# Stage 1 in row halves for two quarters, the last quarter's second stage in two halves, and a new order of issue

## The chip, the cores and the metric

The kernel runs on one core of a Trainium2 chip. A core has five engines with an instruction stream each: TensorE (PE in the profile, with its weight loads listed apart as PEld), VectorE (DVE), ScalarE (ACT), GpSimd (POOL) and SyncE (SP), which issues DMA transfers here. An engine works through its stream in order; between engines, semaphores say when a result is there or a buffer is free. The metric is the time of one execution on the device in microseconds, the median of several runs.

## The reference

Two layers in sequence, on 2048 positions of 512 channels, everything in float32:

```python
def _A_ref(u, ...):                       # S4D: a long convolution per channel
    P = exp((A * dt[:, None])[:, :, None] * pos)          # 512 x 128 x 2048, complex
    K = 2.0 * einsum("dn,dnl->dl", C, P).real             # the kernel of 2048 taps
    y = irfft(rfft(u_t, 2 * L) * rfft(K, 2 * L), 2 * L)[:, :, :L]
    return y + u * D_skip
def _B_ref(x, w_q, k1, k2, u, v):         # PEER: one expert of 256 for each of 32 heads
    q = einsum("nd,dhc->nhc", x, w_q)                     # 2048 x 32 x 256
    s1, s2 = q[..., :128] @ k1.T, q[..., 128:] @ k2.T     # 16 scores each
    e = argmax(s1) * 16 + argmax(s2)
    act = gelu(einsum("nd,nhd->nh", x, u[e]))
    return einsum("nh,nhd->nd", act, v[e])
h  = x + _A_ref(layernorm(x), ...)
h2 = h + _B_ref(layernorm(h), ...)
```

With one candidate per head the softmax is 1. The convolution of both layers' input needs all positions, so the second layer starts when the convolution is through.

## The kernel before, in words

**The first layer** runs over four quarters c of 128 channels, and within them over 32 chunks i of 16 channels (eight to a quarter, two to a piece kt of 32 channels).

For each chunk the taps are made from tables: P at position 64a + b is a product of a coarse power and a fine one. POOL adds the phases as integers (`pg`, in `phases`), and multiplies out the magnitudes (`mg` and `gf`, in `mags` and `tails`); for every fourth chunk it also makes the powers that the next four chunks need (`steps`, `bases`). ACT takes the sines and cosines of the phases into PSUM tiles `t`, named by k (0 coarse, 1 fine) and cosine or sine, DVE multiplies them onto the magnitudes, and PE sums over the 128 states (`kgen`, the tile `kps`: called the product of a chunk below). The tables `pg`, `mg` and `gf` have two buffers each: POOL may write the magnitudes of chunk i when the product of chunk i − 2 has been read.

The Fourier transforms are factored into two stages of matrix products, made for the taps (k) and for the input (u). Stage 1 (`stage1`, tiles s1u and s1k) takes a piece of 32 channels: eight groups g of four channels, 32 rows each, lie on the 128 partitions, and each group is multiplied with two constant matrices `c1_s[:, k]` (real and imaginary part) of 128 by 128, block-diagonal in the four channels. Two plan entries per piece make four groups each, and ACT copies each result (a PSUM bank) into the spectrum `yu` or `yk`:

```python
for k in range(2):
    T.matmul(ps[64 * k:64 * k + 64, g, :], lhs8(4 * n + g), c1_s[:, k], start=True, stop=True)
```

Each of these matmuls of float32 leaves two records in the trace: eight matmuls per entry, 16 records. Stage 2 (`stage2`, tiles s2u and s2yk) has eight operations k4 per quarter, each four matmuls of 128 by 128 (8 records) over the whole spectrum of the quarter, so it needs all four pieces of stage 1. The result for u is copied by ACT into `U`; the result for k is multiplied with `U` by DVE (`prod`). In the last quarter (c = 3) the last of three partial products is left to POOL (`rest`), which reads a copy that ACT makes (`part`). The inverse transform starts with `ia` (`k_ia`): eight operations n of 16 records, each over four groups of channels and the products of all k4. ACT (in the last quarter DVE too) turns the results into the tile `T`, and for the first three quarters SP stores it to DRAM (`t_d`).

In between, PE also projects the second layer's weights onto its keys: 32 pieces n (`w_piece`: the load of `wq` by SP, the product `wps`, a copy `wt`, a transposition `wpt`, a copy into `wh`, and a store per four pieces). The seven PSUM banks of the pool `psA` are shared by stage 1, stage 2, `ia`, the trigonometry and the projections.

**The second layer** runs over the positions: the inverse transform's second part (`ib`), the layer norm with a square on ACT, a product on PE and a sum `vs` on POOL, then for each half the scores (`sc`), the largest of 16 on DVE, the experts' activations, the counts and the output.

**The order.** Nothing is scheduled while the kernel is built: every step is an entry of a plan, with its engine, its dependencies and its buffers, and the table `ORDER` lists the 1728 entries by number. `Plan.run` issues them in that order, so each engine's stream is the table filtered by engine:

```python
for n in order:
    assert n not in done and done.issuperset(self.ops[n][4])
    done.add(n)
    self.ops[n][3]()
```

## Time and profile before

| | us |
|---|---|
| median of three runs (504.18 to 505.11) | 504.2 |
| the profiled execution | 504.94 |
| its span, first to last instruction | 503.2 |
| PE busy | 449.0 (89%) |
| weight loads busy (beside PE) | 390.3 (78%) |
| DVE busy | 407.8 (81%) |
| POOL busy | 325.5 (65%) |
| ACT busy | 298.3 (59%) |

Durations are worked out within the one profiled execution. In the rows of the profile, a time at the row's start is the start in microseconds from the beginning of the span, followed by the duration; then come the engine, the line of the kernel, the operation, and the output tile with `<-` its inputs. A bracket at the end says how long the engine had been idle just before and whose work ended that. In rows that group instructions, busy time and mean duration stand behind the bar, and idle time and its releaser behind the next. An instruction of PE overlaps the next one, so an operation's cost is read from the time between the first and last of its records, not from one record's duration.

Three places of the span matter here: the tables and products up to 263 us, the tail of the last quarter up to 298 us, and the second layer behind it.

### The profile page before, as it was taken

Reading aid. Unit: us, or ns where it says so; the run is one execution under the profiler, and the core shown is the slowest. Engines: PE = TensorE matmul, PEld = TensorE weight load, DVE = VectorE, ACT = ScalarE, POOL = GpSimd, SP = SyncE. Lnnn points to the kernel's source line nnn. Section 1 sums busy time; section 2 is a strip of 40 time slices with the busy share of each in tenths; the row PEclk is TensorE's granted clock in tenths of the full one; section 3 lists DMA queues with packets and bytes.
Section 4 is the critical chain, followed back from the end, with each engine's and each line's share of the span. In section 5 each row is a group of like instructions: output and inputs, shape, how many; then the busy total and the mean of one; then the engine's idle time right before and its main releaser. Section 6 shows DMA issues by size and latency. Waiting matters only on the chain.

```text
span 503.2 us, 16702 instructions
## 1 busy us (share of the span) xinstructions
PE 449.0 (89%) x7206; PEld 390.3 (78%) x7206; DVE 407.8 (81%) x708; ACT 298.3 (59%) x594; POOL 325.5 (65%) x344
## 2 busy tenths in 40 slices
PE   0266879999998999999998889999999999999985
PEld 0144568888997999889997787877878888787874
DVE  5998998899968998899745574888979686978984
ACT  4867799967987588967965362644043430416230
POOL 4989989999999999997824303572163516536130
PEclk9998799999999999999999899999999999999999
DMA  8959474234033300631017689310171311010012
GB/s 253 403 198 381 143 288 148 66 86 179 2 111 124 85 3 1 212 126 45 1 61 259 200 275 283 127 61 1 57 227 55 109 63 43 1 44 0 1 68 62
DMA packets 27362, 61.05 MB, mean 121 GB/s; under 512 B 7028, under 2 KB 14456, under 8 KB 26136
## 3 DMA queue, kind: packets, MB, share of 16 engines
q1 hardware_dynamic: 27136, 59.85, 34.9%
q8 instruction: 57, 0.93, 0.7%
q10 hardware_dynamic: 152, 0.13, 0.1%
q14 instruction: 17, 0.14, 0.1%
HBM read 46.08 MB, written 13.89 MB: 119 GB/s over the span
## 4 chain that ended last, share of the span: by engine, by line
PE 50%; DVE 22%; ACT 10%; POOL 10%; issue 4%; DMA 3%; SPq 1%; ACTq 0%; DVEq 0%; POOLq 0%
PE sc L1150 12%; PE ia L764 9%; DVE oh L1280 5%; PE s2yk L488 3%; PE xu L1157 3%; PE kps L690 3%; PE s2yu L488 3%; POOL pg L557 3%; PE s1u L471 3%; DVE st L232 2%; PE o L1327 2%; PE ib L1036 2%; PE cnt L1290 2%; ACT t L645 2%; POOL mg L594 2%
## 5 line engine op out<-in xcount | busy, mean ns | idle before, releaser
L557 POOL TENSOR_TENSOR pg<-PS 128x1024 int32<-128x1024 int32 x32 | 68.8, 2150 | 0.5
L588 POOL TENSOR_TENSOR mg<-TS 128x1024 f32<-128x1024 f32 x32 | 62.6, 1958 | 7.2 <-PE kps L690 4.5
L1280 DVE TENSOR_SCALAR oh<-idxb,ec_s 128x2048 bf16<-128x2048 bf16 (+1 forms) x72 | 50.3, 757 | 6.8 <-ACT idxb L1262 6.8
L764 PE MATMUL ia<-ca_s,U 128*128 128x128 f32 x256 | 50.6, 280 | 0.4 <-POOL U L743 0.4
L1060 POOL TENSOR_TENSOR vs<-hc 128x256 f32<-128x256 f32 x8 | 7.0, 872 | 62.6 <-ACT hc L1083 62.6
L1192 POOL TENSOR_TENSOR ks<-kq 128x512 f32<-128x512 bf16 x16 | 17.2, 1078 | 45.9 <-DVE kq L1186 44.8
L645 ACT ACTIVATE t<-t,halfpi 128x512 f32<-128x512 f32 x64 | 42.4, 662 | 2.1
L1150 PE MATMUL sc<-w_hi,hhi 128*128 128x480 f32 x128 | 42.4, 412 | 0.0
L644 ACT ACTIVATE t<-pg 128x512 f32<-128x512 int32 x64 | 38.9, 609 | 3.2 <-DVE gf L652 2.2
L764 PEld LDWEIGHTS ia<-ca_s,U 128*128 128x128 f32 x256 | 39.8, 196 | 0.6 <-POOL U L743 0.6
L647 ACT ACTIVATE t<-pg 128x512 f32<-128x512 int32 x64 | 38.2, 608 | 2.8 <-POOL pg L557 1.5
L764 PE MATMUL ia<-ca_s,yk 128*128 128x128 f32 x192 | 38.1, 280 | 0.4 <-DVE mg L664 0.4
L1150 PE MATMUL sc<-w_lo,hhi 128*128 128x480 f32 x128 | 38.4, 380 | 0.0
L1150 PE MATMUL sc<-w_hi,hlo 128*128 128x480 f32 x128 | 38.3, 380 | 0.0
L594 POOL TENSOR_TENSOR mg<-TS 128x512 f32<-128x512 f32 x32 | 37.4, 1170 | 0.4
L690 PE MATMUL kps<-mg 128*32 128x64 f32 x1024 | 34.0, 230 | 3.8 <-DVE mg L664 2.2
L488 PE MATMUL s2yk<-yk,c_s 128*128 128x128 f32 x256 | 34.7, 282 | 1.1 <-ACT yk L474 0.7
L471 PE MATMUL s1u<-c_s,xs 128*64 128x128 f32 x512 | 33.3, 277 | 2.5 <-DVE xs L508 1.6
L690 PE MATMUL kps<-gf 128*32 128x64 f32 x1024 | 33.7, 229 | 1.8 <-issue 1.8
L488 PEld LDWEIGHTS s2yk<-yk,c_s 128*128 128x128 f32 x256 | 30.6, 191 | 4.2 <-issue 1.4
L488 PE MATMUL s2yu<-yu,c_s 128*128 128x128 f32 x256 | 32.6, 279 | 0.3
L471 PEld LDWEIGHTS s1u<-c_s,xs 128*64 128x64 f32 x512 | 27.6, 137 | 5.4 <-DVE xs L508 1.7
(198 smaller groups left out, 1377.5 us busy)
## 6 DMA issues: line engine op xcount, KB each, us to landing
wq<-wq SPq DMA_DIRECT2D x25, 512.0 KB, 4.5
t_d<-T SPq DMA_DIRECT2D x24, 256.0 KB, 3.4
Tb<-t_d SPq DMA_DIRECT2D x8, 768.0 KB, 6.0
x<-xa SPq DMA_DIRECT2D x8, 512.0 KB, 5.6
xs<-xb SPq DMA_DIRECT2D x16, 256.0 KB, 5.3
xt<-xt SPq DMA_DIRECT2D x8, 512.0 KB, 4.8
out<-ob SPq DMA_DIRECT2D x7, 512.0 KB, 3.0
c_s<-wq SPq DMA_DIRECT2D x4, 512.0 KB, 8.3
```

Source lines behind the costliest of these rows:

```text
L471: T.matmul(ps[64 * k:64 * k + 64, g, :], lhs8(4 * n + g), c1_s[:, k], start=True, stop=True)
L488: T.matmul(ps[:, k, :], c2_s[:, kk, :], y[:, :, kk, :], start=True, stop=True)
L557: G.tensor_tensor(view(pg, 0, [[32, 2 * NC], [8, 4], [1, 8]]), view(t["PS"], 1024 + off, [[1, 2 * NC], [128, 4], [0, 8]]), view(t["PS"], 8 ...
L588: G.tensor_tensor(view(mg, 0, [[96, NC], [8, 8], [1, 8]]), view(ts, 512 + 8 * o, [[8, NC], [1, 8], [0, 8]]), view(ts, 8 * o, [[8, NC], [0, ...
L594: G.tensor_tensor(view(mg, 64, [[96, NC], [8, 4], [1, 8]]), view(ts, 1536 + o, [[1, NC], [64, 4], [0, 8]]), view(ts, 1024 + 8 * o, [[8, NC ...
L644: A.activation(p, pg[:, :, k], AF.Abs)
L645: A.activation(p, p, AF.Sin, scale=-SINSCALE, bias=halfpi)
L647: A.activation(p, pg[:, :, k], AF.Sin, scale=SINSCALE)
L690: T.matmul(kps[32 * q:32 * q + 32, 2 * g + h, :], m[:, d, 64:96], m[:, d, 0:64], start=(e == 0), stop=(e == 1))
L764: T.matmul(ps[:, g, :], t[:, 4 * n + g].rearrange("p a b -> p (a b)"), ca_s[:, s, :], start=(s == 0), stop=(s == 1))
L1150: T.matmul(ps[:, 512 * h:512 * h + 480], t[x_][:, q, ts], I[w_][:, q, 480 * h:480 * h + 480], start=(q == 0 and x_ == w_), stop=(q == 3 an ...
L1280: V.tensor_scalar(oh[:, :, 0:ln], t["idxb"][:, :, sl], S["ec"][:, 4 * e + j:4 * e + j + 1], None, op0=ALU.is_equal)
```

## The change

**Stage 1 in row halves.** For quarters 2 and 3, of u and of k, a piece's two entries become two entries of 32 records. Each matmul takes half of the rows (64, two channels of the four) against a constant of 64 by 64, so that the four combinations of row half h and part k lie on four quarters of the PE array. The results of a row half, the channels 2h and 2h + 1 of each group, go to a bank of their own; both banks are taken with the first entry, and ACT copies them out when the second is through. `c1_s` gets 64 more columns per part for this (the load grows from 128 to 192 KB).

**The last quarter's stage 2 in halves of the channels.** With `SEGS[3] = 2`, the eight operations of `k_s2` for c = 3 take eight of the 32 frequencies kk and half of the channels each: 8 matmuls of 128 weights by 64 moving elements. The first four need only the pieces kt 0 and 1 of stage 1, the last four the pieces 2 and 3, and `ia` n = 0 to 3 need only the products of the first four. The input's stage 2 stays whole.

**The order of issue.** Nearly the whole table is new, though some engines begin as before: PE's stream is the same up to its 46th plan entry, ACT's up to its 89th.

```diff
-    16, 0, 2, 1, 17, 18, 4, 23, 80, 3, 5, 9, 7, 24, 65, 19, 26, 20, 180, 21, 22, 10, 34, 6, 183, 35, 36, 197, 29, 185,
+    16, 17, 0, 2, 1, 18, 23, 4, 19, 24, 80, 20, 26, 180, 22, 21, 29, 3, 34, 5, 9, 28, 35, 25, 7, 36, 31, 58, 6, 183, 65,
...
-    c1_s = wk.tile([P, 2, 128], F32, name="c1_s")
+    c1_s = wk.tile([P, 2, 192], F32, name="c1_s")
...
+    SEGS = (1, 1, 1, 2)
...
+    HALF = dict(u=(2, 3,), k=(2, 3,))
+
+    def stage1_rows(dst, lhs8, kt, nm, r, tiles, key):
+        job, k = {}, None
+        for n in range(2):
+            def mm(n=n, job=job):
+                if n == 0:
+                    for h in range(2):
+                        bank(job, f"{nm}_{h}", h)
+                for g in range(4 * n, 4 * n + 4):
+                    for k in range(2):
+                        for h in range(2):
+                            hs = slice(64 * h, 64 * h + 64)
+                            T.matmul(flat(job[h], 64)[64 * k:64 * k + 64, g], lhs8(g)[hs], c1_s[hs, k, 128:192],
+                                     start=True, stop=True)
+
+            k = plan.add("PE", 0.56, mm, r=r, t=tiles, take=() if n else ("psA", "psA"), after=[k] if n else [], n_mm=32)
+        for h in range(2):
+            def ev(h=h, job=job):
+                A.copy(dst()[:, 8 * kt:8 * kt + 8, :, 2 * h:2 * h + 2],
+                       flat(job[h], 64).rearrange("p g (k d) -> p g k d", d=2))
+
+            plan.add("ACT", 0.54, ev, w=[key + (kt, h)], t=tiles, give="psA", after=[k])
+
     def stage1(dst, lhs8, kt, nm, r, tiles, key):
+        if key[1] in HALF[key[0][1]]:
+            return stage1_rows(dst, lhs8, kt, nm, r, tiles, key)
         for n in range(2):
...
-                        T.matmul(ps[64 * k:64 * k + 64, g, :], lhs8(4 * n + g), c1_s[:, k], start=True, stop=True)
+                        T.matmul(ps[64 * k:64 * k + 64, g, :], lhs8(4 * n + g), c1_s[:, k, 0:128], start=True, stop=True)
...
     def k_s2(c):
         plan.group = f"k2{c}"
-        deps = [("yk", c, kt, n) for kt in range(4) for n in range(2)]
+        ns = SEGS[c]
...
         for k4 in range(8):
-            job, k = stage2(c, "yk", k4, deps + u_k + [("U", c, k4)], tiles)
...
+            sg, nk = k4 * ns // 8, 4 * ns
+            g_, k_ = slice(32 * sg // ns, 32 * (sg + 1) // ns), slice(nk * (k4 % (8 // ns)), nk * (k4 % (8 // ns)) + nk)
+            kts = range(4 * sg // ns, 4 * (sg + 1) // ns)
+            deps = [("yk", c, kt, n) for kt in kts for n in range(2)]
...
+            def mm(job=job, g_=g_, k_=k_, k4=k4, nk=nk):
+                ps = flat(bank(job, f"s2yk{c}_{k4}"), 512 // nk)
+                for kk in range(k_.start, k_.stop):
+                    T.matmul(ps[:, kk - k_.start, :], c2_s[:, kk, :], spectrum(c, "yk")[:, g_, kk, :], start=True, stop=True)
...
+            k = plan.add("PE", 0.98 if ns == 1 else 1.15, mm, r=deps + u_k + ["c2"], t=tiles, take="psA", n_mm=8 * ns)
...
     def k_ia(c):
         plan.group = f"ia{c}"
-        deps = [("P", c, k4) for k4 in range(8)]
         for n in range(8):
-            job = {}
+            job, sg = {}, n * SEGS[c] // 8
+            deps = [("P", c, k4) for k4 in range(8 * sg // SEGS[c], 8 * (sg + 1) // SEGS[c])]
```

What the table moves is shown at three places. The names below are those of the tiles with their buffer's number at the end; the digits ahead of it are the quarter and the operation (`s2yk2_3` is stage 2 of k, quarter 2, k4 = 3).

**PE ahead of the product of chunk 26.** Before, these rows stand in a row, a few rows behind the product of chunk 25 and right ahead of that of chunk 26:

```order
L488 MATMUL s2yk2_2_3431<-yk2_3123,c2_s_85 128x128 x4
L488 MATMUL s2yu3_2_3443<-yu3_3045,c2_s_85 128x128 x4
L488 MATMUL s2yu3_7_3452<-yu3_3045,c2_s_85 128x128 x4
L488 MATMUL s2yk2_3_3460<-yk2_3123,c2_s_85 128x128 x4
L488 MATMUL s2yu3_0_3468<-yu3_3045,c2_s_85 128x128 x4
L488 MATMUL s2yk2_5_3474<-yk2_3123,c2_s_85 128x128 x4
L828 MATMUL wps25_3484<-wq25_3157,ka_s_76 32x128 x4
L828 MATMUL wps25_3484<-wq25_3157,kb_s_77 32x128 x4
L488 MATMUL s2yu3_4_3493<-yu3_3045,c2_s_85 128x128 x4
L488 MATMUL s2yk2_1_3507<-yk2_3123,c2_s_85 128x128 x4
L488 MATMUL s2yu3_1_3521<-yu3_3045,c2_s_85 128x128 x4
```

Now, right ahead of the first of projection 31 and the product of chunk 26:

```order
L868 MATMUL wps28_3662<-wq28_3605,ka_s_76 32x128 x4
L868 MATMUL wps28_3662<-wq28_3605,kb_s_77 32x128 x4
L758 MATMUL s2yk2_0_3684<-yk2_3187,c2_s_85 128x128 x4
L876 MATMUL wpt28_3698<-ident_60,wt28_3671 128x128
L868 MATMUL wps29_3700<-wq29_3591,ka_s_76 32x128 x4
L868 MATMUL wps29_3700<-wq29_3591,kb_s_77 32x128 x4
L515 MATMUL s2yu3_1_3711<-yu3_2874,c2_s_85 128x128 x4
L758 MATMUL s2yk2_1_3723<-yk2_3187,c2_s_85 128x128 x4
L758 MATMUL s2yk2_7_3738<-yk2_3187,c2_s_85 128x128 x4
L876 MATMUL wpt29_3743<-ident_60,wt29_3709 128x128
L515 MATMUL s2yu3_4_3746<-yu3_2874,c2_s_85 128x128 x4
L515 MATMUL s2yu3_0_3765<-yu3_2874,c2_s_85 128x128 x4
```

Of the stage-2 operations and stage-1 entries that stood between the products of chunks 25 and 26 (thirteen and five), six and two are left; pieces 28, 29 and 31 of the projections, which stood behind the last product, have come in.

**PE behind the last product.** Before, from the product of chunk 31 on:

```order
L471 MATMUL s1k3_2_0_4008<-c1_s_84,k3_2_3840 64x128 x8
L471 MATMUL s1k3_1_0_4018<-c1_s_84,k3_1_3649 64x128 x8
L471 MATMUL s1k3_3_0_4030<-c1_s_84,k3_3_4001 64x128 x8
L471 MATMUL s1k3_3_1_4040<-c1_s_84,k3_3_4001 64x128 x8
L488 MATMUL s2yk3_0_4050<-yk3_3952,c2_s_85 128x128 x4
L488 MATMUL s2yk3_1_4060<-yk3_3952,c2_s_85 128x128 x4
L488 MATMUL s2yk3_2_4072<-yk3_3952,c2_s_85 128x128 x4
L488 MATMUL s2yk3_3_4079<-yk3_3952,c2_s_85 128x128 x4
L828 MATMUL wps28_4089<-wq28_4070,ka_s_76 32x128 x4
L828 MATMUL wps28_4089<-wq28_4070,kb_s_77 32x128 x4
L488 MATMUL s2yk3_4_4103<-yk3_3952,c2_s_85 128x128 x4
L836 MATMUL wpt28_4108<-ident_60,wt28_4101 128x128
```

Now two stage-2 operations of u and the row-half entries of the last two pieces stand behind that product, with the first two operations of stage 2 among them, and then:

```order
L758 MATMUL s2yk3_2_4409<-yk3_4240,c2_s_85 128x64 x8
L758 MATMUL s2yk3_3_4424<-yk3_4240,c2_s_85 128x64 x8
L758 MATMUL s2yk3_4_4438<-yk3_4240,c2_s_85 128x64 x8
L758 MATMUL s2yk3_6_4447<-yk3_4240,c2_s_85 128x64 x8
L758 MATMUL s2yk3_5_4456<-yk3_4240,c2_s_85 128x64 x8
L758 MATMUL s2yk3_7_4465<-yk3_4240,c2_s_85 128x64 x8
L804 MATMUL ia3_0_4509<-ca_s_86,yu3_2874 128x128
L804 MATMUL ia3_0_4509<-ca_s_86,U3_3716 128x128
```

The projection pieces are gone from here, and `ia` of the last quarter stands right behind the last stage-2 operation.

**ACT around the last cosine of the tables (`t11_31`).** Before:

```order
L644 ACTIVATE t01_31_3845<-pg31_3773 128x512
L645 ACTIVATE t01_31_3845<-t01_31_3845,halfpi_62 128x512
L832 COPY wt26_3897<-wps26_3888 128x128
L832 COPY wt27_3908<-wps27_3899 128x128
L840 COPY wh6_3403<-wpt26_3910 128x120
L840 COPY wh6_3403<-wpt27_3913 128x120
L772 COPY T2_3668<-ia2_1_3819 128x128x4
L772 COPY T2_3668<-ia2_7_3831 128x128x4
L644 ACTIVATE t11_31_3948<-pg31_3773 128x512
L645 ACTIVATE t11_31_3948<-t11_31_3948,halfpi_62 128x512
L474 COPY yk3_3952<-s1k3_0_1_3917 128x512
L772 COPY T2_3668<-ia2_3_3757 128x128x4
```

Now:

```order
L674 ACTIVATE t10_31_4111<-pg31_4069 128x512
L812 COPY T2_3953<-ia2_7_4074 128x128x4
L812 COPY T2_3953<-ia2_3_4083 128x128x4
L671 ACTIVATE t01_31_4150<-pg31_4069 128x512
L672 ACTIVATE t01_31_4150<-t01_31_4150,halfpi_62 128x512
L671 ACTIVATE t11_31_4184<-pg31_4069 128x512
L672 ACTIVATE t11_31_4184<-t11_31_4184,halfpi_62 128x512
L812 COPY T2_3953<-ia2_5_4097 128x128x4
L812 COPY T2_3953<-ia2_6_4153 128x128x4
L483 COPY yk3_4240<-s1k3_0_0_4189 128x256x2
```

The four copies of projection pieces 26 and 27 that stood ahead of the last sine and cosine (`t11_31`) are gone from here, and it follows `t01_31` directly.

More of the change, by code (lines that the diff above doesn't have):

```diff
@@ L735, in prod, with part, rest @@
                     V.tensor_mul(uv[0:64], pv[64:128], uv[0:64])
-            def part(job=job, k4=k4):
-                job["ki"] = wk.tile([P, 128, 4], F32, tag="kt", name=f"ki{k4}", bufs=3)
-                A.copy(job["ki"][0:64], job["ps"].rearrange("p k m -> p m k")[64:128])
-            def rest(job=job, k4=k4):
-                uv = four(c, Q[c]["U"], k4).rearrange("p g d k -> p (g d) k")
+            def part(job=job, k4=k4, nk=nk):
+                job["ki"] = wk.tile([P, 512 // nk, nk], F32, tag="kt", name=f"ki{k4}", bufs=3)
+                A.copy(job["ki"][0:64], flat(job["ps"], 512 // nk).rearrange("p k m -> p m k")[64:128])
+            def rest(job=job, views=views):
+                pv, uv, kv = views()
                 G.tensor_tensor(uv[0:64], job["ki"][0:64], uv[0:64], op=ALU.mult)
+            k = plan.add("PE", 0.98 if ns == 1 else 1.15, mm, r=deps + u_k + ["c2"], t=tiles, take="psA", n_mm=8 * ns)
             if c < 3:
-                plan.add("DVE", 2.14, prod, r=[("U", c, k4)], w=[("P", c, k4)], t=tiles, give="psA", after=[k])
+                plan.add("DVE", 2.14, prod, r=u_k, w=[("P", c, k4)], t=tiles, give="psA", after=[k])
             else:
@@ L750, in k_s2 @@
                 a = plan.add("ACT", 0.52, part, w=[ki], t=[ki], after=[k])
-                v = plan.add("DVE", 1.43, prod, r=[("U", c, k4)], t=tiles, give="psA", after=[k, a])
+                v = plan.add("DVE", 1.43, prod, r=u_k, t=tiles, give="psA", after=[k, a])
                 plan.add("POOL", 1.5, rest, r=[ki], w=[("P", c, k4)], t=[ki, f"U{c}"], after=[v])
```

28 lines of the change are left out of this document (16 added, 12 removed), and 160 rows, old and new, of the table ORDER.

## Prediction

> **What bounds the kernel now.** I read the busy time by stretches first, then POOL's own waits, then the chain of waits from 205 us to 300 us, then the engines around the last table, then the end. The columns of the first view are the stretch, its length, the busy time with instruction counts of PE, PEld, DVE, ACT and POOL, the granted clock, the DMA share and GB/s.
>
> ```profile
> 76.00:231.00 155.00, 151.42 (x2831) 139.54 (x2831) 136.91 (x225) 125.41 (x240) 150.22 (x144) 1.00 0.28 93
> 231.00:256.00 25.00, 24.63 (x443) 23.47 (x444) 20.83 (x36) 21.51 (x40) 19.09 (x12) 1.00 0.08 23
> 256.00:298.00 42.00, 38.36 (x556) 35.24 (x547) 22.20 (x41) 24.29 (x53) 10.11 (x8) 0.96 0.69 226
> 298.00:475.00 177.00, 173.06 (x2232) 144.14 (x2230) 142.16 (x197) 64.53 (x108) 76.41 (x101) 1.00 0.24 79
> ```
>
> From 76 to 231 us POOL (the tables) and PE are both above 96% busy. From 231 on POOL falls to 76% and PE does not: POOL now waits for PE. From 256 to 298 PE works off what is left of the last quarter, and from 298 on PE carries the second half. The change touches the first three stretches; the fourth is touched by order alone. POOL's rows at the end of the tables:
>
> ```profile
> 234.28 1.96 POOL L588 TENSOR_TENSOR mg<-TS 128x1024 f32<-128x1024 f32 x1 [2.78 <-PE kps L690]
> 240.78 1.95 POOL L588 TENSOR_TENSOR mg<-TS 128x1024 f32<-128x1024 f32 x1 [1.31 <-PE kps L690]
> 252.16 1.95 POOL L588 TENSOR_TENSOR mg<-TS 128x1024 f32<-128x1024 f32 x1 [1.05 <-issue]
> 254.08 1.16 POOL L594 TENSOR_TENSOR mg<-TS 128x512 f32<-128x512 f32 x1
> ...
> 143.00:254.10 111.10, 107.87 (x2027) 100.39 (x2026) 95.64 (x156) 89.78 (x169) 103.14 (x94) 1.00 0.24 80
> ```
>
> The buffer that POOL writes (`mg`, two of them) is free once PE has multiplied the chunk two before it. Three times PE was late, 5.14 us in all; POOL is done with the last table at 255.24. The third wait has no named releaser, but it ends just after the product at 251.08 + 1.03 below. The last row, in the first view's columns, runs from the second table of chunk 16 to that of chunk 31: 111.1 us, less the waits 106.0, for fifteen chunks, 7.1 a chunk. Why PE was late is in the chain of waits:
>
> ```profile
> 213.92 0.89 PE kps L690 x64
> 215.91 1.02 PE s1u L471 x16
> 229.80 0.57 PE wps L828 x16
> 232.36 0.89 PE s2yu L488 x8
> 233.25 1.03 PE kps L690 x64
> 245.52 5.55 PE ia L764 x48
> 251.08 1.03 PE kps L690 x64
> 267.61 4.92 DMA wq<-wq
> 272.66 0.65 PE wps L828 x16
> 281.84 15.98 PE ia L764 x126
> ```
>
> Between the products of chunks 25 and 26 (214.81 and 234.28) 19.5 us pass on PE: thirteen stage-2 operations, five of stage 1, a projection and the product itself. The same rows give the prices used below: 0.9 to 1.0 us for a stage-1 operation of 16 records, 0.9 for one of stage 2 (8 records), 1.03 for a product, 1.85 for one `ia` (16 records, a third of 5.55), 0.57 for a projection piece.
>
> **The change, part by part.**
>
> *Stage 1 in row halves.* Sixteen records of 128 rows by 64 columns with 128 moving elements become 32 of 64 by 64 with 64 elements, into two banks. No row shows two row halves at once. The bounds: with every record as long as now (0.87/16 = 0.054 us) 32 make 1.74 us; at the pace of the product `kps` (64 records of 64 elements in 1.03 us, four column tiles at once, 16 ns each) they make 0.51. I take 0.52, since `kps` is the nearest row: also four tiles at once, also 64 moving elements. The Trainium skill ("TensorEngine Tiling (Array Packing)", Instruction Overhead) says each matmul has about 60 cycles of overhead and that no tiling factor should be taken from an already small dimension; at its 2.4 GHz that is an estimated 25 ns a record, 0.80 us an operation, and the end would come at 498 instead of 494.5. Here the trace disagrees, with 16 ns a record in `kps`. The evacuations stay two per piece on ACT, the same 512 elements; both wait for both matmul operations and hold two banks, which is covered by the seven banks.
>
> *PE before the last product.* From the product of chunk 16 to that of chunk 31 PE now does 29 stage-1, 32 stage-2, 16 `ia`, 15 products and 6 projection pieces with transposes: 29×0.9 + 32×0.92 + 16×1.85 + 15×1.03 + 4.1 = 104.7 us. After: 6×0.9 + 26×0.52 + 30×0.92 + 29.6 + 15.5 + 6.8 = 98.4, because stage 1 gives 10 us, the eight pieces of the last projection group move in from behind (2.7) and two stage-2 operations move out. The order spreads it: between the products of chunks 25 and 26 stand two row operations, six of stage 2, three projection pieces and four transposes, 9.7 us with the product instead of 19.5, 2.6 more than POOL's mean chunk, which two buffers hold. So I let all three waits of POOL go: −5.1 us (bounds 0 and −5.6, with the 0.4 us that POOL waited earlier). POOL ends its tables at 250.1; it is late next itself, with no waits left, and is then what cannot be shortened.
>
> *From the last table to the last product.*
>
> ```profile
> 253.82 0.66 ACT L645 ACTIVATE t<-t,halfpi 128x512 f32<-128x512 f32 x1
> 257.41 0.27 ACT L832 COPY wt<-wps 128x128 f32<-128x128 f32 x1 [2.93 <-PE wps L828]
> 261.00 0.69 DVE L664 TENSOR_TENSOR mg<-mg,t 128x512 f32<-128x512 f32 x1 [3.77 <-ACT t L645]
> 262.87 0.29 PE L690 MATMUL kps<-gf 128*32 128x64 f32 x8
> ```
>
> ACT stood 2.93 us behind a projection copy whose PE work was queued behind `ia`, and the last cosine of chunk 31 waited behind it; the last product ended at 263.16, 7.9 us after POOL. In the new order no projection copy stands there, and the cosine follows the one before it. Then DVE's four-step chain counts from POOL's end: 0.68 + 1.28 + 1.28 + 0.68 = 3.9, the product 1.03 and hand-overs 0.2: 5.1. So −2.8, bounds 0 and −3.5; the last product ends at 255.2.
>
> *The last quarter in halves.* Each of the eight stage-2 operations becomes 16 records of 64 moving elements with full 128-column weights. The nearest rows:
>
> ```profile
> 59.36 0.52 PEld L242 LDWEIGHTS mu<-st,eq 128*128 128x128 f32 x4 [0.60 <-ACT t L645]
> 59.39 0.68 PE L242 MATMUL mu<-st,eq 128*128 128x64 f32 x4 [0.39 <-DVE st L232]
> 276.87 0.69 DVE L732 TENSOR_TENSOR yu<-s2yk,U 128x512 f32<-128x512 f32 x1 [0.36 <-ACT ki L739]
> 277.60 0.68 DVE L733 TENSOR_TENSOR U<-s2yk,U 64x512 f32<-64x512 f32 x1
> 280.53 1.26 POOL L743 TENSOR_TENSOR U<-ki,U 64x512 f32<-64x512 f32 x1 [0.18 <-DVE yu L732]
> L739 ACT COPY ki<-s2yk 64x512 f32<-64x512 f32 x8 | 4.7, 583 | 4.3 <-PE s2yk L488 3.9 <-POOL U L743 0.4
> ```
>
> These four loads of 128 columns, also with 64 moving elements, start (0.52 − 0.19)/3 = 0.11 us apart, as those of stage 2 do with 128. So a half operation is 16×0.11 = 1.8 us, not 0.9: +7.1 us for the eight. The other end would be half the moving time, 0.9 and nothing added; I take 1.8, the row. Now the eight operations wait for the products on DVE (0.72×2 each, 11.5 us) and POOL (1.26), and `ia` starts at 281.8 when the last is through. In the new order the first four `ia` need the first half alone: PE goes from stage 2 straight into `ia`. DVE at 1.44 a piece keeps ahead of PE at 1.8. PE's list behind the last product is 2 stage-2 (1.8), 4 row operations (2.1), 8 halves (14.4), 8 `ia` (14.8): 33.1 us without a hole, where now 34.6 (263.16 to 297.80) pass with 4 projection pieces and the 1.3 us that PE waited for `wq` at 272.66 in it. So −1.5, bounds −8.6 and +1.
>
> *Elsewhere.* `c1` grows from 128 to 192 KB in a load of the first microseconds, needed only by the first stage 1 (57 us by the operations' order): nothing. The last `wq` loads and the store of their result move ahead of `ia2`'s stores on SP's queue, where the 4.92 us of the chain fall away; `w_q` loads then have 30 us until the scores. In the second half PE's work is the same and the order new. ACT has two more table loads; the row for one is 1.28 us.
>
> ```profile
> 313.73 1.28 ACT L1128 ACT_TABLE_LOAD   x1 [5.96 <-PE var L1124]
> 315.18 1.04 ACT L983 CAST u_hi<-u_raw 128x1024 fp32r<-128x1024 f32 x1
> 307.89 1.14 POOL L1060 TENSOR_TENSOR vs<-hc 128x256 f32<-128x256 f32 x1 [26.11 <-ACT hc L1083]
> u_raw<-ue SPq DMA_DIRECT2D x1, 512.0 KB, 7.6
> 492.13 0.42 DVE L1299 TENSOR_TENSOR actT<-cnt,actT 128x256 f32<-128x256 f32 x1 [2.37 <-PE ta L1227]
> 496.49 0.42 DVE L1299 TENSOR_TENSOR actT<-cnt,actT 128x256 f32<-128x256 f32 x1 [0.77 <-PE cnt L1290]
> ```
>
> ACT is 36% busy there, so I charge 0.7 of their 2.6 us (bounds 0 and 2.6). At the very end DVE stands still 2.37 us ahead of the first half's weighting; the eight comparisons of the second half (3.2 us) now stand in that place: −1.0 (bounds 0 and −2.4).
>
> Sum: −5.1 − 2.8 − 1.5 + 0.7 − 1.0 = −9.7 against this execution's 504.94 (span 503.2, 1.7 around it): 495.2. The median of the runs, 504.2, lies 0.7 lower, so 494.5.
>
> **Rivals.**
>
> *The row halves bring nothing.* The Trainium skill ("TensorE: Matmul & The Clock Gate", LDWEIGHTS) says that a weight load's time goes with its columns, not its rows: twice the loads of the same 64 columns. If only the column tiles overlap, 32 records take as long as 16 do now, 0.9 us. For it: no row of row halves. Against: loads of 32 columns overlap fourfold in `kps`. Thirty operations at 0.38 more are 11.4, POOL's slack before chunk 31 (106.0 us of POOL's work against 98.4 on PE, less 1.1 of waiting for tables) takes 6.5: 4.9 later, 499.5.
>
> *The row halves take turns.* Nothing overlaps, 1.74 us each: 30×1.22 = 36.6 less 6.5, so 30 later: 525, slower. It decides from 1.0 us an operation, where 30×0.5 − 6.5 = 8.5 eats nearly all the gain. Against it: column tiles already overlap today (s1 at 54 ns a record, `ia` with twice the columns at 116).
>
> *The second half gives it back.* ACT's cast of `u` now stands ahead of the last square of the first block, and waits for a load that can start only when the last quarter is out (7.6 us to land). That square frees POOL's variance sum (307.89, 10 us after `ia`), and PE's variance product now stands ahead of the rest of the first scores. Up to 5 us: 499.5; it would need 10 to be slower.
>
> *Halves at half the load.* If 16 records cost 1.15 us, PE's tail is 5.2 shorter: 489.5. The L242 rows speak against it.
>
> **How the numbers follow.** My forecast 0.52 (own range 491.5 to 497.5); nothing from rows 0.12; turns 0.11; second half 0.16, of which 0.04 slower and 0.03 at no change; cheap halves 0.09. 489 to 501.5 leaves out the turns and the worse end of the second half. Less than 0.2% (1 us) cannot be told from no change. Faster: 0.52 + 0.12 + 0.09 + 0.09 = 0.82; no change 0.03; slower 0.11 + 0.04 = 0.15.
>
> **What would show it.** Row operations of stage 1: 32 records in 0.5 us; above 0.8 the first rival holds. POOL without waits on `kps` between 225 and 252 and its last table near 250. Stage 2 of the last quarter at 1.8 us an operation, `ia` behind it without a hole, ended near 288. First scores some 9 to 10 us earlier than 307. What would make it wrong: a new POOL wait in the tables, or PE gaps ahead of the first scores.

## The result and the profile after

The changed kernel takes 504.49 us (median of 20 runs, 503.24 to 507.27), the kernel before 504.19 (20 runs, 501.98 to 509.37). The ratio is 1.000, with a 95% interval from 0.998 to 1.002: no change. The forecast was 494.5.

The marks of the two profiled executions, beside what the prediction's terms make of them, in us from the start of the span:

| | before | forecast | after |
|---|---|---|---|
| POOL's last table ended | 255.24 | 250.1 | 255.44 |
| last product (chunk 31) ended | 263.17 | 255.2 | 264.24 |
| last `ia` of the last quarter ended | 297.80 | 288.3 | 297.33 |
| first scores started | 307.03 | 297 | 305.17 |
| span | 503.2 | 493.5 | 503.5 |

Of the 10 us by which the forecast is missed, 5.3 are there when the tables end and 9.0 at the last product. The same four stretches as in the prediction, after the change (columns as there: the stretch, its length, PE, PEld, DVE, ACT, POOL with instruction counts, granted clock, DMA share, GB/s):

```profile
76.00:231.00 155.00, 145.78 (x3258) 132.55 (x3255) 133.44 (x221) 128.02 (x249) 149.48 (x144) 0.99 0.33 108
231.00:256.00 25.00, 24.00 (x446) 22.44 (x446) 22.22 (x37) 20.49 (x41) 19.57 (x12) 1.00 0.05 14
256.00:298.00 42.00, 40.91 (x689) 39.65 (x688) 26.03 (x45) 23.43 (x46) 10.12 (x8) 1.00 0.58 184
298.00:475.00 177.00, 171.52 (x2229) 143.73 (x2230) 147.10 (x197) 66.09 (x108) 79.93 (x101) 1.00 0.23 74
```

From 76 to 231 us PE is busy 145.78 us instead of 151.42: the row halves did take work off PE. But PE now stands still for the 9.2 us that are left, and POOL's work is where it was. POOL's waits at the tables (start, duration, engine, line, operation, tiles, and in brackets the idle time and who ended it):

```profile
216.12 1.95 POOL L615 TENSOR_TENSOR mg<-TS 128x1024 f32<-128x1024 f32 x1 [1.32 <-PE kps L717]
234.22 1.96 POOL L615 TENSOR_TENSOR mg<-TS 128x1024 f32<-128x1024 f32 x1 [2.20 <-PE kps L717]
242.07 1.95 POOL L615 TENSOR_TENSOR mg<-TS 128x1024 f32<-128x1024 f32 x1 [2.67 <-PE kps L717]
254.28 1.16 POOL L621 TENSOR_TENSOR mg<-TS 128x512 f32<-128x512 f32 x1
```

Before, the three waits were 5.14 us in all, now they are 6.19: partly at other chunks, and no less. And the chain of waits that ended last, in the same part as before (start, duration, engine, tile, line):

```profile
230.34 0.60 DVE gf L678
...
237.63 0.61 DVE yk L771
...
238.96 0.70 DVE U L774
...
239.80 1.13 PE s2yu L515 x8
240.93 0.11 PE wpt L876
241.04 1.03 PE kps L717 x64
242.07 3.77 PE ia L804 x32
...
260.24 2.02 PE s1k L477 x128
262.26 0.68 PE kps L717 x34
...
272.12 10.86 PE s2yk L758 x96
282.99 14.36 PE ia L804 x128
```

Before, this chain ran through PE alone between the products of chunks 25 and 26. Now it runs through DVE from 230 to 239.7 us, and then through PE without a hole worth naming (0.66 us in the last product) up to the end of the first layer. What DVE does there are the multiplications onto the tables (`gf`, `mg`) and the products of quarter 2 (`yk`, `U`: stage 2 of the taps times `U`). The inverse of quarter 2 needs all eight of these; it starts at 242.0.

The first view again, from 213 to 242 us and from 242 to 264, before:

```profile
213.00:242.00 29.00, 28.40 (x464) 26.11 (x463) 27.93 (x45) 21.06 (x41) 24.28 (x25) 1.00 0.24 74
242.00:264.00 22.00, 21.89 (x473) 20.56 (x473) 12.06 (x22) 16.83 (x34) 12.19 (x8) 1.00 0.09 31
```

and after:

```profile
213.00:242.00 29.00, 25.45 (x612) 21.79 (x610) 26.72 (x42) 21.43 (x46) 22.25 (x22) 1.00 0.32 98
242.00:264.00 22.00, 21.34 (x515) 20.35 (x512) 14.80 (x26) 18.16 (x34) 13.37 (x8) 1.00 0.12 41
```

Already before, DVE was busy 27.93 of these 29 us, nearly as much as PE. After, PE has 3.55 us of idle time in it and DVE 2.28. From 242 on PE is 97% busy or more in both. PE's own waits ahead of 242 name the engine:

```profile
217.19 1.16 PE L758 MATMUL s2yk<-yk,c_s 128*128 128x128 f32 x8 [0.81 <-DVE mg L687]
222.71 0.33 PE L876 MATMUL wpt<-ident,wt 128*128 128x128 f32 x1 [1.24 <-DVE U L774]
224.62 0.61 PE L868 MATMUL wps<-wq,ka_s 128*32 128x128 f32 x7 [0.49 <-ACT t L672]
239.80 1.13 PE L515 MATMUL s2yu<-yu,c_s 128*128 128x128 f32 x8 [0.96 <-DVE U L774]
```

The first two and the last read nothing that DVE writes there (stage 2 of the taps and of `u`, a transposition of projection weights). What they share with DVE's operands is the pool of seven PSUM banks.

### The profile page after: what moved, and what is told of

The parts are those of the page before. It is cut to its first block, busy times and chain, and to the rows that moved or that the text cites. A ratio compares the mean times of both kernels' runs of the same rounds, so it can differ in the third digit from the quotient of the medians.

```text
span 503.5 us, 17847 instructions
## 1 busy us (share of the span) xinstructions
PE 445.1 (88%) x7782; PEld 387.8 (77%) x7782; DVE 412.5 (82%) x708; ACT 301.1 (60%) x596; POOL 327.9 (65%) x344
## 4 chain that ended last, share of the span: by engine, by line
PE 59%; DVE 20%; POOL 9%; ACT 7%; issue 3%; DMA 2%; SPq 0%; POOLq 0%; DVEq 0%; ACTq 0%
PE sc L1190 11%; PE ia L804 10%; PE s2yk L758 6%; PE s2yu L515 5%; PE o L1367 4%; DVE oh L1320 4%; PE kps L717 4%; PE xu L1197 3%; POOL pg L584 2%; DVE st L233 2%; PE ib L1076 2%; PE cnt L1330 2%; PE s1k L498 2%; POOL mg L621 2%; PE s1u L498 2%
## 5 line engine op out<-in xcount | busy, mean ns | idle before, releaser
L1320 DVE TENSOR_SCALAR oh<-idxb,ec_s 128x2048 bf16<-128x2048 bf16 (+1 forms) x72 | 52.1, 781 | 5.9 <-ACT idxb L1302 5.6
L804 PE MATMUL ia<-ca_s,U 128*128 128x128 f32 x256 | 49.5, 275 | 0.0
L758 PE MATMUL s2yk<-yk,c_s 128*128 128x128 f32 (+1 forms) x320 | 40.8, 278 | 0.9 <-DVE mg L687 0.8
L758 PEld LDWEIGHTS s2yk<-yk,c_s 128*128 128x128 f32 x320 | 37.6, 192 | 2.5 <-DVE mg L687 1.0
L515 PEld LDWEIGHTS s2yu<-yu,c_s 128*128 128x128 f32 x256 | 30.2, 192 | 3.8 <-PE s2yk L758 1.1
L717 PEld LDWEIGHTS kps<-mg 128*32 128x32 f32 x1024 | 25.1, 114 | 10.2 <-issue 2.9
```

Of the source, the lines that this page charges most:

```text
L515: T.matmul(ps[:, k, :], c2_s[:, kk, :], y[:, :, kk, :], start=True, stop=True)
L717: T.matmul(kps[32 * q:32 * q + 32, 2 * g + h, :], m[:, d, 64:96], m[:, d, 0:64], start=(e == 0), stop=(e == 1))
L758: T.matmul(ps[:, kk - k_.start, :], c2_s[:, kk, :], spectrum(c, "yk")[:, g_, kk, :], start=True, stop=True)
L804: T.matmul(ps[:, g, :], t[:, 4 * n + g].rearrange("p a b -> p (a b)"), ca_s[:, s, :], start=(s == 0), stop=(s == 1))
L1320: V.tensor_scalar(oh[:, :, 0:ln], t["idxb"][:, :, sl], S["ec"][:, 4 * e + j:4 * e + j + 1], None, op0=ALU.is_equal)
```

## The experiments

The theories that the expectations name. A is the prediction's: the tables set the pace, and PE counts where POOL waits for it. B: PE's own work from 143 to 298 us sets the end of the first layer. C: the row halves cost in waits what they save. D, formed after the first eight runs: from 213 us on DVE is the full engine, the last product of quarter 2 sets when its inverse starts, and only what PE saves behind that point (242 us) counts.

All kernels are the changed kernel with its two switches, `HALF` and `SEGS`, and a table `ORDER`; e8, e9 and e12 also change the products on DVE. "Old order" is the sequence of before, "new order" that of the changed kernel, both by name of entry. The results, with the marks of each profiled execution (start of quarter 2's inverse, end of the last product, end of the first layer's `ia`, first scores; us). The runs of before that went with them had medians of 503.4 (e1 to e4), 505.2 (e5 to e8), 504.6 (e9 to e12) and 504.8 (e13, e14); the ratios are to these. The marks are those of one execution each: e10's took 522.9 us and e9's 512.9, 6.1 and 2.4 above their medians, and the others lie within 2.3 us of theirs.

| kernel | median | ratio to before (95%) | inverse 2 | last product | `ia` end | scores |
|---|---|---|---|---|---|---|
| before | 504.2 | | 237.6 | 263.2 | 297.8 | 307.0 |
| after | 504.5 | 1.000 (0.998 to 1.002) | 242.0 | 264.2 | 297.3 | 305.2 |
| e1 rows, old order | 512.5 | 1.017 (1.014 to 1.020) | 244.4 | 270.5 | 307.3 | 315.5 |
| e2 halves, old order | 508.7 | 1.010 (1.006 to 1.013) | 237.3 | 262.9 | 300.0 | 308.6 |
| e3 new order alone | 513.5 | 1.019 (1.015 to 1.022) | 241.9 | 264.8 | 302.0 | 311.6 |
| e4 rows and halves, old order | 517.7 | 1.028 (1.024 to 1.031) | 244.9 | 270.6 | 309.2 | 317.7 |
| e5 after without rows | 506.3 | 1.002 (1.000 to 1.005) | 241.9 | 264.8 | 299.5 | 307.4 |
| e6 after without halves | 514.2 | 1.018 (1.015 to 1.022) | 241.8 | 264.3 | 301.2 | 312.3 |
| e7 projections behind the tables | 512.7 | 1.013 (1.009 to 1.018) | 239.2 | 261.9 | 298.0 | 310.4 |
| e8 after, less DVE | 504.2 | 0.999 (0.996 to 1.002) | 241.3 | 263.4 | 297.3 | 306.0 |
| e9 after, more DVE | 510.5 | 1.013 (1.010 to 1.016) | 246.5 | 270.6 | 304.6 | 312.8 |
| e10 rows, old order, placed early | 516.8 | 1.029 (1.024 to 1.034) | 246.9 | 275.4 | 310.2 | 322.4 |
| e11 second layer in old sequence | 515.5 | 1.022 (1.018 to 1.025) | 242.0 | 264.3 | 298.2 | 306.1 |
| e12 e7, less DVE | 506.4 | 1.003 (1.000 to 1.005) | 236.5 | 257.8 | 294.5 | 305.6 |
| e13 rows in last taps, old order | 505.7 | 1.002 (1.000 to 1.005) | 238.4 | 263.7 | 300.0 | 308.2 |
| e14 after, rows in last taps only | 504.3 | 0.999 (0.998 to 1.001) | 240.7 | 263.4 | 296.5 | 304.4 |

**Each part alone.** First the row halves in the old order:

```diff
-    SEGS = (1, 1, 1, 2)
+    SEGS = (1, 1, 1, 1)
...
     HALF = dict(u=(2, 3,), k=(2, 3,))
```

> Stage 1 in row halves for quarters 2 and 3, everything else as before (a piece's two entries stand together at the place of the later one). 32 operations, some 0.38 us shorter each, 11 to 12 us of PE time in all. Theory A (the tables set the pace and PE counts only where POOL waits for it): of the 5.1 us of POOL's waits some 3 go and the four operations behind the last product give 1.5: 499.5 to 500.5. Theory B (PE's own work and its holes from 143 to 298 us set the end of the first layer): the whole saving comes out, less holes where PE then waits for DVE: 493 to 497.

It was 512.5, slower by 1.7%: both theories missed by more than 10 us. PE waited, in the view of who waited for whom from 143 to 275 us (total us, times, longest):

```profile
PE s1k L477 <- DVE gf L679: 2.8, 2, 1.6
PE s2yu L515 <- ACT yu L483: 2.4, 2, 1.2
PE kps L717 <- DVE mg L691: 2.2, 1, 2.2
PE s1u L477 <- DVE U L774: 1.7, 2, 1.0
```

PE's holes of over 0.1 us between 143 us and the last product grew from 3.3 to 15.7 us in all, more than the 11 that the operations save. L477 is the row entry itself, and it waits for DVE's `gf` and `U`, which it does not read: the first entry of a piece takes two banks at once. The Trainium skill ("TensorEngine Tiling (Array Packing)", Gotcha 1: PSUM Pressure) says that row tiles must write different banks and so raise the pressure on PSUM; it gives no price. In this order the form costs 9 us net.

The halves in the old order:

```diff
-    HALF = dict(u=(2, 3,), k=(2, 3,))
+    HALF = dict(u=(), k=())
...
     SEGS = (1, 1, 1, 2)
```

> The last quarter's stage 2 in halves of the channels, everything else as before. Eight operations of 1.8 instead of 0.9 us add 7.1 us of PE time behind the last product; the holes that the products left there (about 2 of the 3.5 us) close. Both theories: 508 to 510. At 504 or less the halves would pay by themselves.

508.7: as expected. Its `ia` ends 2.2 us later than before.

The new order without the two edits:

```diff
-    SEGS = (1, 1, 1, 2)
+    SEGS = (1, 1, 1, 1)
...
-    HALF = dict(u=(2, 3,), k=(2, 3,))
+    HALF = dict(u=(), k=())
```

> The new order of issue with stage 1 and stage 2 as before (eleven entries brought forward where their dependencies ask for it). Theory A: the earlier last cosine and fewer waits of POOL give about 5, the hole ahead of the last quarter's inverse, no longer filled by projections, takes some 5: about 504. Theory B: PE's work is that of before and the new order adds its holes (4.7 us in the tables, some 2 in the second layer) and the one of some 5 us in the tail: 511 to 516.

513.5, in theory B's range and far from A's. But the last product is at 264.8, where the changed kernel has it (264.2), though all of stage 1 is whole: not what B says. The loss is in the tail, where nothing stands any more beside the products of the last quarter:

```profile
PE ia L804 <- DVE yu L771: 6.1, 1, 6.1
```

Both edits in the old order (`HALF` and `SEGS` as in the changed kernel):

> Both edits of PE's work with the old order of issue. Both theories: the sum of the two kernels that have one of them, about 504.2 + (rows alone - 504.2) + (halves alone - 504.2); theory B 497 to 503, theory A 503 to 506. Below 504.2 the new order is what costs the gain.

517.7, and the single differences to the same runs of before give 503.4 + 9.1 + 5.3 = 517.8: the two edits add up in the old order, both as losses.

**One part undone.** In the new order, stage 1 whole again:

```diff
-    HALF = dict(u=(2, 3,), k=(2, 3,))
+    HALF = dict(u=(), k=())
```

> The changed kernel with stage 1 whole again in quarters 2 and 3. Theory A (the tables set the pace): some 5 slower than the changed kernel, 509. Theory B (PE's work sets the first layer's end): 30 operations at 0.38 us come back in full, less the waits for banks that the row halves caused: 511 to 516. Rival C (in the new order too the row halves cost in waits for two banks what they save): 503 to 506.

506.3, 0.2% above before: 32 operations that are 0.4 us longer cost 1 to 2 us. Theories A and B both fall, and C's range is the nearest. The stretches of this kernel:

```profile
143.00:213.00 70.00, 69.42 (x1334) 64.32 (x1334) 57.11 (x94) 56.97 (x110) 66.86 (x60) 1.00 0.30 103
213.00:242.00 29.00, 28.00 (x554) 24.27 (x552) 26.66 (x42) 22.07 (x48) 24.85 (x26) 1.00 0.35 102
```

Against the changed kernel PE is busy 2.55 us more from 213 to 242; DVE is busy 26.66 instead of 26.72, the same work at the same place. The inverse of quarter 2 starts at 241.9 instead of 242.0. The 2.2 us by which `ia` ends later (299.5 against 297.3) are the row operations behind 242.

> The changed kernel with the last quarter's stage 2 whole again (eleven entries brought forward). PE's work falls by 7.1 us, and a hole of about 6 us opens ahead of the last inverse, as in the kernel with the order alone (6.07): all theories within 2 us of the changed kernel, 502 to 506.

The edit is `SEGS = (1, 1, 1, 1)`. All theories missed: 514.2. The 6.07 us hole ahead of `ia` came as expected, and `ia` ends 3.9 us later than in the changed kernel. I had left out what follows: the inverse of the whole layer then waits again, and the first scores start 7.2 us later.

```profile
PE ia L804 <- DVE yu L771: 6.1, 1, 6.1
PE ib L1076 <- issue: 3.0, 1, 3.0
PE s2yk L758 <- ACT yk L483: 1.7, 1, 1.7
```

So in the new order the halves are worth 9 us, and the new order alone costs 10. The row halves bring nothing here either: e3, without them, takes 1.019 of before, this kernel, with them, 1.018.

**Which engine is full.** In the new order up to the last product, the last four projection pieces go back behind it (everything behind in the old order, stage 2 whole):

> Row halves and the new order up to the last product of the tables, but the last four projection pieces back behind it, stage 2 of the last quarter whole, and everything behind that product in the order of before. Theory B: 3.4 us of projections leave PE's list ahead of the last product and fill the hole behind it; first layer ended 1 to 3 us earlier than before, and the second layer as before: 500 to 503. Theory A: POOL's waits ahead of chunks 28 and 29 (2.2 and 2.7 us) shrink by the 3.4 us and the last cosine is early: 497 to 500.

The last product came 2.3 us earlier (261.9 instead of 264.2) and `ia` ended where it did before, but the kernel takes 512.7, some 10 us above the ranges of both theories: PE then has 12 us of holes in the second layer instead of 7 to 8, which I didn't follow up. For the tables it says that the projections there do cost time. The pieces are 3.4 us of PE's work ahead of 242 us, and without them the inverse of quarter 2 starts 2.8 us earlier (239.2): for these, the last clause of theory D, that only what PE saves behind that point counts, does not hold.

DVE's products, one of three left out:

```diff
-                if c < 3:
+                if c < 2:
                     V.tensor_mul(uv[0:64], pv[64:128], uv[0:64])
```

> The changed kernel, leaving out the third of the three partial products on DVE in quarter 2 (eight of some 0.7 us, 5.6 us of DVE in all); its output is not the reference's. If PE's holes between 215 and 240 us (0.81, 1.24 and 0.96 us) are waits for banks that DVE's products of quarter 2 hold, most of these 3 us go and the end of the first layer comes 2 to 4 us earlier: about 501. If PE is late by its own list alone, the time stays within 1 us of the changed kernel's.

504.2: by the expectation PE would be late by its own list alone. The hole at 239.8 is gone, though two of 0.72 and 1.43 us stay ahead of 225.5, and from there to 262 us PE has none: its list with the projections in it is now as long as DVE's, and the inverse of quarter 2 starts only 0.7 us earlier. One engine relieved isn't enough to tell, so DVE was loaded instead:

```diff
-                V.tensor_mul(kv, pv, uv)
+                for _ in range(2 if c == 2 else 1):
+                    V.tensor_mul(kv, pv, uv)
```

> The changed kernel with the first partial product of quarter 2 multiplied twice on DVE (eight more multiplications of some 0.7 us, 5.6 us, all between 213 and 242 us; the output stays the reference's). Theory D: from 213 us on DVE is the full engine, the last product of quarter 2 (241.8) sets when the inverse of quarter 2 starts, and from there PE has no hole up to the second layer: the first layer and the whole end 4 to 6 us later, 508 to 510. Theory A (POOL's tables with PE's list set the pace): DVE has room, within 1.5 us of the changed kernel.

510.5, 5.9 above before for 5.6 us of DVE: theory D, just above its range. The last product of quarter 2 and the inverse behind it, in this kernel's rows of DVE and PE:

```profile
244.93 1.42 DVE L772 TENSOR_TENSOR yk<-s2yk,U 128x512 f32<-128x512 f32 x2
...
246.49 0.46 PE L805 MATMUL ia<-ca_s,yk 128*128 128x128 f32 x2
...
270.32 0.32 PE L717 MATMUL kps<-gf 128*32 128x64 f32 x6
```

The inverse starts 4.5 us later and the last product ends 6.4 later, so DVE has no room there. Part of the two distances is this execution's own: it lies 2.4 us above the median, and behind a wait of PE for DVE the clock was granted at 0.57 from 225 to 229 us. And both relieved together, e7 with the third product left out:

> The kernel with the last four projection pieces behind the tables, leaving out the third partial product of quarter 2 on DVE (5.6 us; output not the reference's). In the changed kernel less DVE work brought only 0.5 us, and PE then had no hole from 225 us on: its list with the projection pieces in it took over. Without these pieces theory D expects the inverse of quarter 2 to start 3 to 5 us earlier than in the kernel with only the pieces moved (239.2 us) and the last product at 257 to 259 instead of 261.9; if POOL sets the pace, both move by less than 1 us.

```profile
236.52 0.49 PE L804 MATMUL ia<-ca_s,yk 128*128 128x128 f32 x2
...
257.51 0.29 PE L717 MATMUL kps<-gf 128*32 128x64 f32 x8
```

The inverse starts 2.7 us earlier than in e7, a little less than expected, and the last product ends at 257.8, as expected. Less DVE alone gave 0.9 us there, the projections alone 2.3, both 6.4. And POOL has no wait left behind 216.29 us; its last row at the tables is

```profile
249.51 1.16 POOL L621 TENSOR_TENSOR mg<-TS 128x512 f32<-128x512 f32 x1
```

so the last table ends at 250.67, where the forecast had 250.1. The waits behind 217 us, which the prediction let go, hang on both, on DVE's products and on the projections that stand among the operations feeding them. Theory D is right that DVE has no room from 213 to 242 us, and too simple: PE's list with the projections has none either. (The time of e12, 506.4, is not a test of the forecast's sum, since its tail is the old one, with stage 2 whole.)

**Where row halves pay.** The second try of e1, with the entries and evictions of a piece placed early:

> The row halves alone in the order of before again, a piece's two entries now at the place of the earlier one and both evictions right behind them. If the 8.5 us that the first such kernel lost came from where its entries were put, this one ends at 503 to 506 (theory D: the saving is lost in PE's holes, but nothing more); if they come from the row form itself, which takes two banks at once, 509 to 514 again.

516.8, above both ranges: the loss isn't due to where the first try put them. That two banks at once are the cause fits the waits, but no kernel took a row form with one bank, so this stays argued.

Row halves for the last taps alone:

```diff
-    HALF = dict(u=(2, 3,), k=(2, 3,))
+    HALF = dict(u=(), k=(3,))
```

> The kernel before with row halves only for the taps of the last quarter (eight operations, from about 250 us on, four of them behind the last product), old order, stage 2 whole. Theory D: PE has no hole in the old order from 238 us to the tail, so what row halves save there counts: eight times 0.38 us, 500.5 to 502.5. If the row form itself costs waits wherever it stands, as in the two kernels with row halves in both quarters, 505 to 508.

> The changed kernel with row halves only for the taps of the last quarter; the other 24 operations of stage 1 are whole again, some 9 us more PE work, all of it ahead of 242 us. Theory D: these 9 us go into PE's holes ahead of the inverse of quarter 2, which starts at 242 as before, and the time is that of the changed kernel within 1 us, 503.5 to 505.5. Theory B (all of PE's work counts): 511 to 514.

In the new order the time is as theory D has it: 504.3, with 24 operations of stage 1 whole again. The inverse of quarter 2 even starts 1.3 us earlier than in the changed kernel, at 240.7. PE is busy 2.55 us more from 213 to 242, and the view of who waited for whom has two lines for PE from 143 to 262 us, where the changed kernel has twelve:

```profile
213.00:242.00 29.00, 28.00 (x543) 24.46 (x542) 27.45 (x44) 22.38 (x48) 24.85 (x25) 1.00 0.33 99
...
PE s2yu L515 <- DVE U L774: 1.0, 1, 1.0
PE s1k L498 <- DVE gf L682: 0.6, 1, 0.6
```

In the old order theory D's number is missed, 505.7 instead of 500.5 to 502.5; it lies in the range for a row form that costs waits wherever it stands (505 to 508). The old order has the last cosine late, and what PE saves ahead of the last product turns into a wait for it; the row entries' evictions are waited for in the tail (PE, then DVE's row that ended the first wait):

```profile
262.56 0.32 PE L717 MATMUL kps<-mg 128*32 128x64 f32 x8 [2.25 <-DVE mg L691]
270.05 3.84 PE L758 MATMUL s2yk<-yk,c_s 128*128 128x128 f32 x32 [1.29 <-ACT yk L483]
...
261.72 0.69 DVE L691 TENSOR_TENSOR mg<-mg,t 128x512 f32<-128x512 f32 x1 [3.77 <-ACT t L672]
```

**The second layer.** Its entries in the sequence of before, on the places that the new order gives to the second layer:

> The changed kernel with the second layer's entries in the sequence of before, on the places that the new order gives to the second layer. In the profiles the second layer took 198.3 us from the first scores to the end in the changed kernel and 196.1 before. If the new sequence costs these 2.2 us, this kernel ends at 502 to 503; if they vary from one execution to the next (the same sequence took 196.2 in the kernel with less DVE work), it stays within 1 us of the changed kernel, 503.5 to 505.5.

515.5: neither. The mixture has a wait of its own:

```profile
PE sc L1190 <- DVE hlo L1120: 6.3, 1, 6.3
```

So this kernel tells nothing about the 2.2 us. The other traces do: from the first scores to the end it took 196.1 us before, 198.3 after, and 196.2, 196.8 and 196.7 in e8, e5 and e14, which have the new sequence too. The last matmuls of the output, in the changed kernel and in e5:

```profile
493.89 5.46 PE L1364 MATMUL o<-actT,v_raw 128*128 128x128 f32 x32
...
496.16 3.84 PE L1364 MATMUL o<-actT,v_raw 128*128 128x128 f32 x32
```

The same 32 records took 1.62 us longer in the changed kernel's execution, where the granted clock was 0.58 from 494 to 498 us; in e5 it was 1.00 from 496 to 500, and e8 and e14 took 3.84 too. So 1.6 of the 2.2 us are a spell of half clock in that one execution and not the order. No kernel was found that beats both.

## Why the prediction was wrong

*The size of a row operation* was right. At full clock four took 2.02 us (the chain's row at 260.24), 0.505 each against 0.52. The rival in which row halves take turns falls, and so does the price of the rival in which they bring nothing (0.9), though most of its outcome came true by another way. The prediction's other estimate, 0.80 us, took 25 ns for each of the 32 records. Measured are 15.8 ns a record, or 32 ns for each of the sixteen matmuls, so whether the rows contradict it depends on whether the overhead counts by record or by matmul, which no run tells; and by the prediction's own slack it would have given 30 × 0.28 − 6.5 = 1.9 us more, 496.4 and not 498. Two other slips leave the sum as it is: by the prediction's own list stage 1 gives 7.2 us up to the last product and not 10, since three more of its operations fall into that stretch, and the projection pieces that move in are four, not eight.

*"So I let all three waits of POOL go"* is the step that failed. Measured, the waits went from 5.14 to 6.19 us. The step set PE's list (98.4 us) against POOL's tables (106.0) and took the difference as slack. Up to 213 us the tables did set the pace (POOL was busy 67.81 of the 70 us from 143 to 213 before and 68.24 after), so there PE's saving could bring next to nothing. Behind that the step left out DVE, which stands between the two: from 213 to 242 us DVE has the products of quarter 2 (eight of 2.1 us) and the multiplications of chunks 25 to 27, and was nearly as full as PE already before (27.93 and 28.40 us). Three kernels in the new order with 0, 8 and 32 row operations (e5, e14, after) start the inverse of quarter 2 at 241.9, 240.7 and 242.0; 5.6 us more on DVE make the kernel 5.9 us slower; and POOL's two waits behind 217 us (2.20 and 2.67) go when DVE's products and the projections are both relieved (e12: last table at 250.67), but stay in part when DVE's products alone (1.31 and 1.46 in e8) or the projections alone are (1.46 and 1.86 in e7). The view was at hand: the prediction's first row for 76 to 231 us averages DVE to 88%, the row for 213 to 242 shows 96%.

*The order around chunk 26* was to put 9.7 us between the two products. It was 13.0 (221.2 to 234.2), of which 1.7 are the waits at 222.71 and 224.62, and the products of quarter 2 ended at 241.8 instead of 236.9, since the projections stand between their stage-2 operations (without them, in e7, the inverse behind these products starts 2.8 us earlier). This is how a gain on PE became a later start of the inverse.

*From the last table to the last product* I took −2.8 us. The mechanism worked: the last multiplication on DVE ended at 259.4 instead of 261.7, as the cosine was early. But PE wasn't there; behind 242 its list (eight `ia` in 15.1 us, three products, four row operations) runs without a break until 262.2. The distance was 8.8 us instead of 7.9, so this term is +0.9. The late cosine had been hidden behind a PE that wasn't free either.

*The halves and the tail* were right to a tenth: 10.86 us for six operations, 1.81 each, and 33.1 us from the last product to the end of `ia`, as worked out, with no hole. The term of −1.5 is there, but partly by luck: `ia` alone took 15.98 us before and 14.36 after, and in the execution of before it ran into this stretch:

```profile
282.00:286.00 4.00, 4.00 (x22) 4.00 (x23) 0.26 (x3) 0.73 (x2) 0.00 (x0) 0.58 0.78 213
```

Without the granted clock of 0.58 the old tail would have taken an estimated 33.0 us, as long as the new one. The prediction showed 0.96 for the whole stretch and priced `ia` at full clock in the new tail only. What I didn't see is how much hangs on it: without the halves the new order has a hole of 6.07 us and takes 9 us longer.

*Elsewhere*: I took −0.3 for what stands behind `ia`; in the profiles it was +0.8. Of that, 1.6 us are the half clock at the end of that execution; without it the term would be an estimated −0.8. The rival in which the second half gives up to 5 us back did not come: the first scores started 1.9 us earlier, and PE's holes from 298 us on are 7.8 us instead of 6.8.

So −5.1, −2.8, −1.5 and −0.3 became +0.2 (last table), +0.9, −1.5 and +0.8, and the sum +0.3 (spans of 503.16 and 503.49). The rivals nearest to the outcome, "the row halves bring nothing" and "the second half gives it back", kept the other terms and so gave 499.5.

## What to carry to other kernels

Time saved on an engine ahead of a point where it waits for another one is lost unless that other engine is relieved too; look for such points before adding up, here the start of an inverse that needs every product of a third engine. Read the busy time of all engines in stretches as short as the hops of the chain: an engine that is 88% busy on the mean of 155 us was 96% busy in the 29 that mattered. An edit that makes an operation shorter but takes more buffers at once can lose more in waits than it saves; the same row halves cost 9 to 12 us in one order and brought at most 2 in another.

## What the runs showed of the hardware

PE's clock can be halved for some microseconds behind a short pause in which PE is not idle, and the same pause can leave it alone. In the changed kernel PE stopped inside a row entry while the DMA engines were 83% busy (rows of PE, then of the stretches; the clock stands behind POOL's count):

```profile
205.53 0.56 PE L477 MATMUL s1k<-c_s,k 64*64 64x64 f32 x18 [0.23 <-ACT wh L880]
207.16 3.25 PE L477 MATMUL s1k<-c_s,k 64*64 64x64 f32 x108 [1.07 <-issue]
...
204.00:207.20 3.20, 1.74 (x81) 1.33 (x73) 2.45 (x5) 3.13 (x7) 3.20 (x3) 1.00 0.83 330
207.20:210.40 3.20, 3.20 (x112) 3.08 (x115) 1.82 (x4) 1.68 (x5) 3.20 (x3) 0.50 0.04 13
```

With PE busy 1.74 of 3.2 us the next 3.2 us were granted at 0.50, and 108 records took 3.25 us, where 128 took 2.02 at full clock. In e11, which has the same order up to there and the same hole of 1.07 us, the clock stayed at 1.00 and the 108 records took 1.85:

```profile
204.80:208.00 3.20, 1.65 (x79) 1.33 (x73) 2.36 (x5) 3.10 (x7) 3.20 (x2) 1.00 0.82 325
208.00:211.20 3.20, 2.73 (x127) 2.26 (x126) 2.44 (x5) 2.34 (x5) 3.20 (x3) 1.00 0.06 21
```

e6 and e12 kept the clock behind this hole too, e9 lost it, so the pause alone does not decide it. It isn't what cost the gain either: the inverse of quarter 2 starts at 242.0 in e11 and at 241.8 in e6. The Trainium skill ("TensorE: Matmul & The Clock Gate", What's actually happening) has PE at half clock after an idle window of some 3.4 us; the spell here lasted as long (0.50 from 207.2 to 210.6), but the window ahead of it was more than half busy. The hole itself is named "issue": no semaphore was waited for, and it stands in the middle of an entry of 64-column records.
